# A short convolution and two matrix products on one core: the opening in a new order on all queues

## The chip, the cores and the metric

The kernel runs on one core of one Trainium2 chip. The core has five engines, each with a queue of its own that is worked off strictly in order: PE (TensorE, matrix products), DVE (VectorE), ACT (ScalarE), POOL (GpSimd) and SP (SyncE, which here only issues DMAs). An instruction at the head of a queue that has to wait holds back all that stands behind it on that queue, and nothing else. DMAs are issued by SP and by POOL. The metric is the device time of one execution in microseconds (us).

## The reference

`x` is 8 x 4096 x 192, `w_in` is 192 x 2048, `w_out` is 2048 x 192, all float32.

```python
w = softmax(weight, axis=-1)                    # 8 heads x 7 taps
conv[b, s, d] = sum_k w[head(d), k] * x[b, s - 6 + k, d]   # causal, 24 channels a head
h = conv.reshape(32768, 192) @ w_in             # 32768 x 2048
g = h * (1 / (1 + exp(-1.702 * h)))
out = g @ w_out                                 # 32768 x 192
```

## The kernel before

**Work in big steps.** The 32768 tokens are worked off in 32 "big steps" (`big` = 0 to 31). Each has 512 tokens from each half of the batch. A big step has three parts: the convolution (7 taps for each of three groups `c` of 64 channels; a tap is a product with one scalar a channel), the first product with the gelu, and the second product with transposition and store. Both products of steps 1 to 31 are done by a fast bilinear scheme: sums of blocks of the convolution (`SUMS_C`), sums of blocks of `w_in` (`SUMS_W`, 24 of them, made once, in place), 20 block products for each half `v` of the columns (`FIRST`, `TERMS`), and for the second product sums of `w_out` ("forms": `COPY_O` copies on ACT, `SUMS_O` adds by POOL's accumulating DMAs, in four stages `add_forms(0)` to `add_forms(3)`, and four sign changes on ACT in `end_forms`) and sums of `g`.

**Step 0 is different** and is called the opening here. While `w_in` and `w_out` still arrive and are rounded (eight pieces: `split_piece` on DVE, `split_rest` on ACT, `join_piece`, `sign_piece` and the rounding on DVE), the first product is done plainly: 16 calls of `plain`, 12 of them in a loop in `first_step`. After each call comes a gelu on ACT and then one function of the list `stages`, in which the rest is hung: the pieces of the weights, the loads, the taps of step 1. The second product of step 0 (`second_first`) uses a scheme of seven products of quadrants: `a11` to `a22` are parts of `w_out`, `b11` to `b22` parts of `g`; `s1` to `s4` and `t1`, `t2` are sums of them, and `sums_b` overwrites `b12` with `b22 - b12`. Each call of `go` takes some steps of a product; one step is four matmuls side by side in the four column groups, three for the main product and one "side" matmul for another (`aside`), and each matmul is two passes. PE's order is: a11 b11 (8 steps), a12 b21 (6), s2 t2 (8), a12 b21 (2), s3 b12 (8), s4 b22 (2), a22 t2 (8); the side matmuls of steps 1 to 24 are s1 t1, those after them s4 b22. Behind the seven products come four transposes on DVE (`turn`) and the stores.

**The convolution of step 1.** Groups 2 and 0 go by `tap`: ACT multiplies each tap into a place of its own, and POOL adds the places up with accumulating DMAs in the order of `TREE_1`; those of one group are (1,2), (3,4), (0,1), (5,6), (0,3), (0,5), of which (0,1), (0,3) and (0,5) each need the landing of the one before. Group 1 goes by `conv` on DVE, handed out by `work(us)` from the list `todo`. `need("done 1")` issues what is left of it, then one sum on DVE (`OPEN_SUM`), which needs all taps of all groups, and then blocks of the convolution are copied across partitions by SP's DMAs (`cross`, `cross_piece`). Only then can the ten sums `SUMS_C` of step 1 be made (`next_sum`); for step 1 they are DVE's, for all later steps POOL's.

**Order by hand.** Nothing reorders at run time. `FILL_1` says what is put between which of the items of `FIRST` in step 1 (a dictionary for `v` = 0 and one for `v` = 1, keys are indices into `FIRST`); `FILL` does so for later steps. `PLAN` is the written order of the second product of steps 1 to 31. `begin_sums(2)` stands behind step 1's first product, so step 2's ten sums are handed out by the `vsum` entries of `PLAN`; for later steps they are all handed out by `FILL` before `PLAN` begins, and the `vsum` entries then find nothing.

Of the kernel before, what the change touches and what calls it, by code (L numbers as in the profile page):

```python
# [15 lines left out]
def kernel(  # L16
# [149 lines left out]
    def side(big, other, b):  # L166
# [4 lines left out]
    SUMS_W = [  # L171
# [4 lines left out]
    ]  # L176
    OPEN_W = 0
# [193 lines left out]
    def sums_w_in(i):  # L371
        add_up(lambda j: w_in_s[:, j, :], *SUMS_W[i])
# [267 lines left out]
    def plain(u, m, n, v, slot, ks=range(NC), first=0):  # L640

        for k in ks:
# [101 lines left out]
    def fill(big, kind, *args):  # L744
        if kind == "work":
            work(*args)
        elif kind == "tap":
            next_tap()
        elif kind == "add":
            for _ in range(*args):  # L750
                next_add()
        elif kind == "vsum":
            next_sum()
        elif kind == "cross":
            cross_piece()
        elif kind == "turn":
# [25 lines left out]
    def second_first(between, fetch, last_seeds):  # L782
# [83 lines left out]
        add_forms(0)  # L866
        sub(t1[1], b12[1], b11[1])
# [22 lines left out]
        act.copy(whole(c12), whole(a))  # L890
        go(c11, p2[6:], first=False)
        sub(t2[0], b21[0], t2[0])
        sub(t2[1], b21[1], t2[1])
        add(p1, p1, whole(c11))
        go(a, listed(s3, b12), first=False)
        add_forms(2)
        between()
        act.copy(whole(c21), whole(a))
        add(p5, p5, whole(a))
        go(c12, p3[6:], first=False)  # L900
        cross_piece()
        for i in range(OPEN_W):
            sums_w_in(i)
        fetch()
        for i in range(OPEN_W, len(SUMS_W)):
            sums_w_in(i)
        next_tap()
        next_tap()
        steps = listed(a22, t2, (1, 0))
        for i in range(0, len(steps), 2):  # L910
            go(c21, steps[i : i + 2], first=False)
            if i == 0:
                last_seeds()
            next_tap()
            if i < 6:
                next_tap()
        assert not side
        cross_piece()
        turn(0, 0, blocks(p1), js)
        cross_piece()  # L920
        assert not pieces
        turn(1, 1, blocks(p5), js)
        add(q12, q12, whole(c12))
        turn(1, 0, blocks(whole(c21)), js)
        store(0, 0)
        turn(0, 1, blocks(q12), js)
        store(0, 1)

# [11 lines left out]
    def store(big, n, o=None, queues=(nc.sync,) * 3):  # L940
# [29 lines left out]
        ("side", 8, 8, "k1", 2, 4), ("acc", 7, 10), ("sum", 13, 18, "+", 4), ("acc", 18, 14), ("main", 2, 5, "p4", 0),  # L970
        ("sum", 6, 9, "-", 5), ("vsum",), ("go", 1), ("tap",), ("go", 2), ("tap",), ("tap",), ("tree",), ("go", 1),
# [5 lines left out]
        ("main", 21, 7, "p2", 0), ("go", 2), ("side", 7, 20, "k1"), ("vsum",), ("tap",), ("tree",), ("go", 2),  # L977
# [375 lines left out]
```

## Time and profile before

| what | value |
|---|---|
| median of 3 runs | 2276.99 us (2276.36 to 2277.63) |
| the profiled execution's own time | 2275.51 us |
| its span, first to last instruction | 2273.7 us |
| mean granted clock of PE | 0.996 |
| PE busy | 2252.5 us (99%) |
| DVE, ACT, POOL busy | 1985.3 (87%), 1709.2 (75%), 1069.9 (47%) us |

The span is 1.8 us shorter than the profiled execution's own time; what lies between is outside of the program's instructions. The busy time of PE includes the overlap of matmuls in flight, so a busy PE isn't a PE at its peak; where PE waits less than a matmul's length, no idle time shows. Start times in the timelines count from the start of the span. In a row of the timeline, a bracket at the end says how long the engine had been idle and what ended the wait; `xN` says that N instructions of the same kind are merged in one row.

### The profile page before, as it was taken

How to read it: one execution, taken by the hardware profiler on the slowest of the kernel's cores; microseconds unless marked ns; L12 is line 12 of the kernel's file. 1: busy time of each engine (PE TensorE's matmuls, PEld its weight loads, DVE VectorE, ACT ScalarE, POOL GpSimd, SP SyncE). 2: the span in 40 equal slices, each digit the busy share in tenths (PEclk: the TensorE clock that was granted, in tenths of full speed). 3: DMA queues.
4: the chain of work that ended last, by engine and by line, in shares of the span. 5: the costliest groups of instructions: out<-in, count | busy, mean ns of one | idle time of the engine just before them, and what ended most of it. 6: DMA issues, size and time to landing. Idle time of an engine off the chain costs nothing.

```text
span 2273.7 us, 62148 instructions
## 1 busy us (share of the span) xinstructions
PE 2252.5 (99%) x24966; PEld 1564.5 (69%) x24966; DVE 1985.3 (87%) x2967; ACT 1709.2 (75%) x3233; POOL 1069.9 (47%) x1101
## 2 busy tenths in 40 slices
PE   9899999999999999999999999999999999999999
PEld 5366577776777667777667776677776677766775
DVE  8798889988889888898888888888988888888888
ACT  8477777778777787777787777877777877778754
POOL 1446544555434555445554445554455544455510
PEclk9899999999999999999999999999999999999999
DMA  8876577666576565776665765666766657665543
GB/s 200 153 152 142 111 141 152 127 128 126 114 162 138 124 132 114 139 153 129 128 126 113 161 139 124 130 117 136 154 130 128 126 112 160 139 126 106 101 97 71
DMA packets 276111, 298.84 MB, mean 131 GB/s; under 512 B 119152, under 2 KB 203376, under 8 KB 275824
## 3 DMA queue, kind: packets, MB, share of 16 engines
q0 software_dynamic: 58080, 151.48, 36.9%
q1 hardware_dynamic: 216096, 142.99, 27.7%
q8 instruction: 198, 3.24, 0.6%
q14 instruction: 89, 0.73, 0.1%
q10 hardware_dynamic: 1648, 0.39, 0.1%
HBM read 53.15 MB, written 25.17 MB: 34 GB/s over the span
## 4 chain that ended last, share of the span: by engine, by line
PE 92%; DVE 4%; DMA 2%; ACT 1%; issue 1%; POOL 0%; DVEq 0%; POOLq 0%; ACTq 0%; SPq 0%
PE slot L597 47%; PE slot L1021 45%; DVE g L363 1%; DMA conv_t<-conv_t 1%; DMA xin<-in_x_dram 0%; PE slot L839 0%; DMA g<-osbs 0%; DMA conv_t<-w_form 0%; DVE room L363 0%; DVE w_in_s L363 0%; DMA w_in_s<-in_moe_w_out_dram 0%; DVE slot L638 0%; DVE osbs L937 0%; DVE conv_t L474 0%; PE slot L1113 0%
## 5 line engine op out<-in xcount | busy, mean ns | idle before, releaser
L597 PE MATMUL slot<-conv_t,w_in_s 64*128 64x512 f32 x5152 | 1148.5, 595 | 2.2 <-DVE slot L638 1.4
L597 PEld LDWEIGHTS slot<-conv_t,w_in_s 64*128 64x128 f32 x5152 | 669.5, 186 | 468.3 <-issue 304.9
L1021 PE MATMUL slot<-g,w_form 128*32 128x256 f32 x9672 | 894.2, 379 | 0.7 <-DVE room L363 0.7
L1021 PEld LDWEIGHTS slot<-g,w_form 128*32 128x32 f32 x9672 | 576.3, 110 | 129.3 <-DVE room L363 1.7
L506 POOL TENSOR_TENSOR conv_t<-conv_t,g 128x512 f32<-128x512 f32 x354 | 450.5, 1279 | 96.5 <-ACT g L488 72.9
L1021 PE MATMUL slot<-g,w_out_s 128*32 128x256 f32 x5952 | 467.5, 379 | 1.1 <-DVE g L363 1.1
L363 DVE TENSOR_TENSOR g<-g 128x1024 f32<-128x1024 f32 x372 | 451.2, 1226 | 7.5 <-DMA g<-osbs 1.0
L1046 ACT COPY room<-slot 32x256 f32<-32x256 f32 x651 | 237.6, 365 | 289.7 <-PE slot L1021 281.4
L638 DVE TENSOR_TENSOR room<-slot,room 128x512 f32<-128x512 f32 x620 | 383.7, 680 | 67.0 <-PE slot L597 66.7
L632 ACT COPY room<-slot 128x512 f32<-128x512 f32 x620 | 337.8, 595 | 75.6 <-PE slot L597 59.1
L488 ACT ACTIVATE g<-xt,cw 128x512 f32<-128x512 f32 x534 | 354.1, 715 | 3.6
L619 ACT ACTIVATE g<-room 128x1024 f32<-128x1024 f32 x248 | 265.6, 1071 | 79.6 <-DVE room L638 50.2
L614 ACT ACTIVATE g<-slot 128x512 f32<-128x512 f32 x528 | 283.1, 609 | 51.5 <-PE slot L597 32.2
L997 POOL DMA_DIRECT2D g<-g x124 | 127.2, 1031 | 360.2 <-PE slot L1021 343.3
L638 DVE TENSOR_TENSOR slot<-slot,room 128x512 f32<-128x512 f32 x372 | 239.8, 689 | 53.9 <-PE slot L597 51.2
L1021 PEld LDWEIGHTS slot<-g,w_out_s 128*32 128x32 f32 x5952 | 239.7, 110 | 41.8 <-DVE room L638 22.8
L361 POOL TENSOR_TENSOR conv_t<-conv_t 128x256 f32<-128x256 f32 x210 | 181.5, 870 | 129.4 <-PE slot L597 120.0
L1021 PE MATMUL slot<-osbs,w_form 128*32 128x256 f32 x2232 | 229.5, 379 | 0.0
L511 POOL DMA_DIRECT2D g<-g x120 | 105.8, 881 | 232.6 <-ACT g L488 91.9
L1021 PEld LDWEIGHTS slot<-osbs,w_form 128*32 128x32 f32 x2232 | 132.4, 110 | 23.8
L638 DVE TENSOR_TENSOR slot<-room,slot 128x512 f32<-128x512 f32 x124 | 79.8, 688 | 43.0 <-PE slot L597 42.0
L1021 PE MATMUL slot<-room,w_form 128*32 128x256 f32 x1488 | 112.9, 379 | 0.4 <-DVE room L363 0.4
(169 smaller groups left out, 1678.7 us busy)
## 6 DMA issues: line engine op xcount, KB each, us to landing
g<-g POOLq DMA_DIRECT2D x124, 512.0 KB, 6.4
xin<-in_x_dram SPq DMA_DIRECT2D x240, 180.0 KB, 4.1
conv_t<-conv_t SPq DMA_DIRECT2D x186, 192.0 KB, 5.4
g<-g POOLq DMA_DIRECT2D x120, 256.0 KB, 5.3
conv_t<-conv_t SPq DMA_DIRECT2D x186, 128.0 KB, 3.0
out_dram<-osbs SPq DMA_DIRECT2D x186, 128.0 KB, 2.7
g<-room POOLq DMA_DIRECT2D x31, 512.0 KB, 5.2
conv_t<-g POOLq DMA_DIRECT2D x60, 256.0 KB, 5.4
```

Source lines behind the costliest of these rows:

```text
L361: eng.tensor_add(v(dst), v(a), v(b))
L363: eng.tensor_sub(v(dst), v(a), v(b))
L488: act.mul(home, conv_src(big, c, k), cw[:, c, k : k + 1])
L506: nc.gpsimd.tensor_add(dst, dst, home)
L597: nc.tensor.matmul(slot[h], w_in_s[halves[h], a, v * P : (v + 1) * P], src, start=first, stop=True, skip_group_check=True,)
L614: act.activation(dst[:, :, h, :], src[h].rearrange("p (o t) -> p o t", o=2), AF.Gelu_apprx_sigmoid, scale=float(sign),)
L619: act.activation(dst.rearrange("p o h t -> p h o t"), src.rearrange("p h (o t) -> p h o t", o=2), AF.Gelu_apprx_sigmoid, scale=float(sign),)
L632: act.copy(bank(dst, h), bank(src, h))
L638: op(*(bank(t, h) for t in (dst, a, b)))
L997: nc.gpsimd.dma_start(out=spot(dst), in_=spot(a), accum_op=ALU.add)
L1021: nc.tensor.matmul(dst, w, t, start=first, stop=last, skip_group_check=True)
L1046: act.copy(to, d)
```

## The change

No instruction of the computation is added or taken away; the order in which they are put on the queues is new, from 28 us of the profile on to the end of step 1.

1. `stages`: the rounding of `w_out`'s pieces and the load and transposes of step 1's input are handed out in another order, so that `round_w_out(1)` stands in front of `turn_x(1)`, and `split(7)` behind the first sum `t1[0]`. The 14 taps of step 1 go 3 into stage 6, 4 into stage 8, 6 into stage 10, 1 into stage 11 (before: 1, 1, 2, 2, 2, 2, 2, 2 in stages 4 to 11).
2. `second_first`: `s3[0]`, `sums_b(0)` and `sums_b(1)` stand in front of `need("done 1")`; `add_forms(0)` and `add_forms(1)` behind it, before the copy of a11 b11 out of PSUM; the ten `SUMS_C` and the 24 `SUMS_W` are spread among the rest (`next_w`), the latter in a new order that keeps their dependences; step 1's first product (`fetch`) stands before the last two steps of s4 b22; two of the transposes change places.
3. `add_forms(2)` moves from `second_first` to the start of step 1's first product, `add_forms(3)` from the end of `first_step` to index 9 of its second half, `end_forms` to index 25 of that half.
4. `FILL_1`: step 2's taps and the group that DVE does (`work`) stand at other indices; 4 of the 7 `conv` of step 2 fall into the first half, 3 into the second (before: all 7 into the first).
5. `PLAN`: the ten `vsum` stand at other places. They act in step 1 alone.

```diff
     SUMS_W = [
-        (12, 2, "+", 5), (13, 7, "-", 10), (11, 13, "-", 11), (12, 11, "+", 12), (14, 8, "+", 11), (15, 1, "-", 11),
+        (12, 2, "+", 5), (13, 7, "-", 10), (11, 13, "-", 11), (18, 13, "-", 0), (15, 1, "-", 11), (16, 0, "+", 9),
...
+    w_left = list(SUMS_W)
+    def next_w(n):
+        for _ in range(n):
+            add_up(lambda j: w_in_s[:, j, :], *w_left.pop(0))
     FILL_1 = [
         {
-            0: (("add", 12),), 1: (("work", 0.8),), 8: (("work", 0.8),), 9: (("tap",),), 16: (("work", 0.8),),
-            19: (("tap",),), 21: (("tap",), ("work", 0.8)), 27: (("work", 0.8),), 28: (("work", 0.8),),
-            30: (("tap",),), 31: (("tap",),), 34: (("tap",),), 42: (("work", 0.8), ("tap",)),
+            0: (("form", 2),), 5: (("tap",),), 6: (("work", 0.8),), 8: (("add", 12),), 9: (("tap",),),
+            14: (("work", 0.8), ("tap",)), 16: (("work", 0.8),), 20: (("tap",),), 25: (("tap",),),
+            28: (("work", 0.8),),
         },
         {
-            5: (("g", 0),), 8: (("g", 1),), 13: (("turn", 0),), 15: (("g", 2),), 19: (("turn", 1),), 20: (("g", 3),),
-            24: (("turn", 2),), 29: (("g", 4),),
+            4: (("g", 0),), 8: (("work", 0.8),), 9: (("form", 3),), 15: (("turn", 0),), 21: (("g", 1),),
+            22: (("turn", 1),), 24: (("turn", 2),), 25: (("forms",),), 27: (("g", 2),), 31: (("g", 3),),
+            37: (("g", 4),),
         },
     ]
# second_first
-        add_forms(0)
+        steps = listed(a22, t2, (1, 0))
+        sub(s3[0], a11[0], a21[0])
         sub(t1[1], b12[1], b11[1])
         add(s1[1], a21[1], a22[1])
+        sub(s2[1], s1[1], a11[1])
+        sums_b(0)
+        sub(s2[0], s1[0], a11[0])
         go(a, listed(a11, b11))
-        act.copy(p1, whole(a))
+        sums_b(1)
         sub(t2[1], b22[1], t1[1])
-        for i in range(2):
-            sub(s2[i], s1[i], a11[i])
-        add_forms(1)
         need("done 1")
         cross_blocks(1)
         while pieces:
             cross_piece()
-        for i in range(2):
-            sub(s4[i], a12[i], s2[i])
-            sub(s3[i], a11[i], a21[i])
+        begin_sums(1)
+        sub(s4[0], a12[0], s2[0])
+        next_sum()
         go(c11, p2[:6], more=True)
-        begin_sums(1)
-        while sums_left:
+        for _ in range(3):
             next_sum()
+        add_forms(0)
+        add_forms(1)
+        sub(s3[1], a11[1], a21[1])
+        act.copy(p1, whole(a))
...
+        go(a, listed(s2, t2), first=False)
...
+        sub(t2[0], b21[0], t2[0])
+        next_sum()
+        sub(s4[1], a12[1], s2[1])
...
+        go(a, listed(s3, b12), first=False)
+        act.copy(whole(c21), whole(a))
         cross_piece()
-        sums_b(0)
-        sums_b(1)
-        go(a, listed(s2, t2), first=False)
...
+        next_w(3)
+        fetch()
+        next_w(2)
         sub(t2[1], b21[1], t2[1])
+        next_w(1)
+        go(c12, p3[6:], first=False)
         between()
-        act.copy(whole(c21), whole(a))
+        next_w(8)
+        next_tap()
...
-        for i in range(OPEN_W, len(SUMS_W)):
-            sums_w_in(i)
...
# first_step: the stages (after)
+        def stage_0():
+            split(4); split(5); load_x(1)
+        def stage_1():
+            rounds(3)
+        def stage_3():
+            round_w_out(0)
+        def stage_4():
+            round_w_out(1); split(6); load_w_out(3)
+        def stage_5():
+            turn_x(1)
+        def stage_6():
+            round_w_out(2); taps_next(3)
+        def stage_8():
+            next(rest); todo.extend(prepare(1)); taps_next(4); split(7)
+        def stage_9():
+            round_w_out(3)
+        def stage_10():
+            taps_next(1); next(rest); taps_next(4); next(rest); taps_next(1)
+        def stage_11():
+            taps_next(1); work(1.3)
...
-        add_forms(3)
         end_taps()
```

More of the change, by code (lines that the diff above doesn't have):

```diff
@@ L755, in fill @@
             cross_piece()
+        elif kind == "forms":
+            need("forms")
+        elif kind == "form":
+            add_forms(*args)
         elif kind == "turn":
@@ L892, in second_first @@
-        sub(t2[0], b21[0], t2[0])
+        add_forms(0)
+        add_forms(1)
+        sub(s3[1], a11[1], a21[1])
+        act.copy(p1, whole(a))
+        for _ in range(2):
+            next_sum()
+        go(a, listed(s2, t2), first=False)
+        for _ in range(2):
+            next_sum()
+        go(c11, p2[6:], first=False)
+        next_sum()
+        sub(t2[0], b21[0], t2[0])
+        next_sum()
+        sub(s4[1], a12[1], s2[1])
+        add(p1, p1, whole(c11))
+        act.copy(whole(c12), whole(a))
@@ L893, in second_first @@
+        next_w(2)
+        go(a, listed(s3, b12), first=False)
+        act.copy(whole(c21), whole(a))
+        cross_piece()
+        next_w(3)
+        fetch()
+        next_w(2)
         sub(t2[1], b21[1], t2[1])
-        add(p1, p1, whole(c11))
-        go(a, listed(s3, b12), first=False)
-        add_forms(2)
+        next_w(1)
+        go(c12, p3[6:], first=False)
         between()
-        act.copy(whole(c21), whole(a))
-        add(p5, p5, whole(a))
-        go(c12, p3[6:], first=False)
@@ L901, in second_first @@
-        cross_piece()
-        for i in range(OPEN_W):
-            sums_w_in(i)
-        fetch()
-        for i in range(OPEN_W, len(SUMS_W)):
[L906 to L917, printed above, removed]
+        next_w(8)
@@ new lines, in second_first @@
+        next_tap()
+        next_w(2)
+        cross_piece()
+        next_w(1)
+        go(c21, steps[0:2], first=False)
+        next_w(3)
+        next_tap()
+        last_seeds()
+        next_tap()
+        go(c21, steps[2:4], first=False)
+        add(p5, p5, whole(a))
+        for _ in range(2):
+            next_tap()
+        go(c21, steps[4:6], first=False)
+        for _ in range(2):
+            next_tap()
+        go(c21, steps[6:8], first=False)
+        for _ in range(2):
+            next_tap()
@@ L918, in second_first @@
+        cross_piece()
+        next_w(1)
+        turn(0, 0, blocks(p1), js)
+        next_w(1)
         cross_piece()
[L919 to L922, printed above, removed]
         add(q12, q12, whole(c12))
         turn(1, 0, blocks(whole(c21)), js)
-        store(0, 0)
+        turn(1, 1, blocks(p5), js)
         turn(0, 1, blocks(q12), js)
         store(0, 1)
+        store(0, 0)
+        assert not side and not pieces and not sums_left
@@ L1239, in first_step, with stage_2, stage_7 @@
         rest = second_first(between, fetch, last_seeds)
+        def stage_0():
+            split(4)
+            split(5)
+            load_x(1)
+        def stage_1():
+            rounds(3)
+        def stage_2():
+            pass
         def stage_3():
+            round_w_out(0)
+        def stage_4():
+            round_w_out(1)
             split(6)
+            load_w_out(3)
+        def stage_5():
             turn_x(1)
-        def stage(n, todo=lambda: next(rest)):
-            todo()
-            taps_next(n)
-        split(3)
-        stages = [
-            stage_0, stage_1, stage_2, stage_3, lambda: stage(1, stage_4), lambda: stage(1, lambda: split(7)),
-            lambda: stage(2, lambda: round_w_out(2)), lambda: stage(2, lambda: round_w_out(3)),
-            lambda: stage(2), lambda: stage(2), lambda: stage(2), lambda: stage(2, lambda: work(1.3)),
-        ]
+        def stage_6():
+            round_w_out(2)
+            taps_next(3)
+        def stage_7():
+            pass
+        def stage_8():
+            next(rest)
+            todo.extend(prepare(1))
+            taps_next(4)
+            split(7)
+        def stage_9():
+            round_w_out(3)
+        def stage_10():
+            taps_next(1)
+            next(rest)
+            taps_next(4)
+            next(rest)
+            taps_next(1)
+        def stage_11():
+            taps_next(1)
+            work(1.3)
+        split(3)
+        rounds(2)
+        load_w_out(2)
+        stages = [stage_0, stage_1, stage_2, stage_3, stage_4, stage_5,
+            stage_6, stage_7, stage_8, stage_9, stage_10, stage_11]
         free = [slots[0], sums, slots[1], slots[2]]
```

26 lines of the change are left out of this document (4 added, 22 removed), and 46 rows, old and new, of tables (PLAN, SUMS_W).

## The prediction

> **What bounds the kernel now.** I read the page first, then the busy time by stretches, then the timelines of PE, DVE, POOL and ACT over the first 190 us.
>
> ```profile
> span 2273.7 us, 62148 instructions
> PE 2252.5 (99%) x24966; PEld 1564.5 (69%) x24966; DVE 1985.3 (87%) x2967; ACT 1709.2 (75%) x3233; POOL 1069.9 (47%) x1101
> 75.00:100.00 25.00, 17.34 (x137) 5.95 (x128) 19.24 (x27) 4.12 (x7) 14.05 (x16) 0.80 1.00 176
> 110.98:187.08 76.10, 72.66 (x780) 46.61 (x779) 72.06 (x100) 55.89 (x106) 36.58 (x34) 1.00 0.79 155
> 187.08:206.00 18.92, 18.66 (x85) 11.67 (x83) 13.65 (x23) 15.91 (x28) 14.21 (x12) 1.00 0.34 72
> 187.08:257.91 70.83, 70.22 (x786) 44.75 (x784) 60.91 (x92) 54.67 (x103) 34.89 (x35) 1.00 0.67 136
> ```
>
> The columns of the stretches are length, then busy time of PE, weight loads, DVE, ACT and POOL, granted clock, DMA share, GB/s. Over the whole span PE is the bound and nothing can be won in the later steps, which the change leaves alone: step 2 (187.08 to 257.91) has PE busy for 70.22 of 70.83 us. It is the opening that isn't bound by PE: from 75 to 100 us PE works 17.34 of 25 us. Step 1 (110.98 to 187.08) takes 5.3 us longer than step 2 and is DVE's: 72.06 of 76.10 us busy.
>
> ```profile
> 18.71 37.18 PE L597 MATMUL slot<-conv_t,w_in_s 64*128 64x512 f32 x172 [0.26 <-DVE w_in_s L346]
> 57.96 0.63 PE L839 MATMUL slot<-g,w_out_s 128*32 128x512 f32 x3 [2.07 <-ACT g L614]
> 80.00 0.59 PE L844 MATMUL slot<-w_in_s,conv_t 128*32 128x512 f32 x1
> 88.25 1.07 PE L839 MATMUL slot<-g,conv_t 128*32 128x512 f32 x3 [7.66 <-DVE g L851]
> 91.04 0.85 PE slot L839 x3
> 93.77 0.43 PE slot L839 x3
> ```
>
> The last two rows are of the chain that ended last. PE ends the plain products at 55.9, begins the seven products at 57.96, does 24 of the 42 steps by 80.6, and then stands for 7.66 us until `sums_b` (L851) has made the new b12. Its first passes after that take 0.85 us, the later ones 0.43, so the gap costs more than its length.
>
> ```profile
> 40.22 2.10 DVE L443 STREAM_TRANSPOSE xt<-xin 128x576 f32<-128x576 f32 x3 [2.11 <-DMA xin<-in_x_dram]
> 50.57 0.95 DVE L338 SCALAR_TENSOR_TENSOR w_form<-osbs,w_form 128x768 uint32<-128x768 uint32 x1
> 51.55 1.44 DVE L346 SCALAR_TENSOR_TENSOR w_out_s<-w_form 128x96 f32<-128x96 f32 x8
> 55.30 2.29 DVE L855 TENSOR_TENSOR room<-g,room 128x2048 f32<-128x2048 f32 x1
> 57.51 0.55 DVE L857 TENSOR_TENSOR w_form<-w_out_s 128x384 f32<-128x384 f32 x1
> 59.95 2.28 DVE L867 TENSOR_TENSOR w_in_s<-g 128x2048 f32<-128x2048 f32 x1
> 65.75 3.11 DVE L474 SCALAR_TENSOR_TENSOR conv_t<-xt,cw,conv_t 128x512 f32<-128x512 f32 x4
> 79.51 0.42 DVE L361 TENSOR_TENSOR conv_t<-conv_t 128x256 f32<-128x256 f32 x1 [10.65 <-DMA conv_t<-conv_t]
> 85.82 4.49 DVE L851 TENSOR_TENSOR g<-g 128x2048 f32<-128x2048 f32 x2
> 98.33 0.68 DVE L899 TENSOR_TENSOR room<-room,slot 96x512 f32<-96x512 f32 x1 [1.01 <-ACT slot L898]
> 110.98 1.24 DVE L638 TENSOR_TENSOR room<-slot,room 128x512 f32<-128x512 f32 x2
> ```
>
> This names the cause. DVE has nothing to do from 68.86 to 79.51: `need("done 1")` puts `OPEN_SUM` at the head of its queue, which waits 10.65 us for the taps' DMAs, and `s3`, `s4`, the ten sums and `sums_b`, which PE needs, are queued behind. After that DVE is busy nearly without a pause to 110.98, where step 1's first sum (L638) begins, and on through step 1. So the path is: taps' DMAs, then DVE.
>
> **The change on that path.** It fills DVE's 10.65 us with work that stood behind them. I work along DVE's queue in four pieces.
>
> *Entry.* ACT's rows are needed here.
>
> ```profile
> 46.13 0.94 ACT L326 ACTIVATE w_form<-w_form,bias 128x768 f32<-128x768 uint32 x1 [2.08 <-DVE w_form L315]
> 51.70 1.34 ACT L488 ACTIVATE w_form<-xt,cw 128x512 f32<-128x512 f32 x2
> 52.92 1.08 ACT L614 ACTIVATE g<-slot 128x512 f32<-128x512 f32 x2
> 53.88 0.74 ACT L488 ACTIVATE w_form<-xt,cw 128x512 f32<-128x512 f32 x1
> 60.42 1.39 ACT L488 ACTIVATE conv_t<-xt,cw 128x512 f32<-128x512 f32 x2
> 69.39 2.99 ACT L405 COPY w_form<-w_out_s 128x384 f32<-128x384 f32 x7
> ```
>
> With `round_w_out(1)` (3.2 us, like L338 and L346 with their join) in front of the transposes, their 2.11 us of wait is covered. It is lost again at piece 7: its ACT half now stands behind stage 8's gelu and four taps. A call of `plain` is 12 matmuls of the 172, 2.6 us, so stage 8's product ends at 55.9 - 3 x 2.6 = 48.1; gelu 1.1, four taps at 0.62 (half of 1.34, less overlap) 2.5, two passes of the piece 1.9: 53.6. Then DVE's sign 1.0, rounding 1.4, `t2[0]` 2.2, `s1[0]` 0.5: 58.7, where it now ends at 58.0. PE's first step needs `s1[0]` for its side matmul, so PE begins 0.9 later, at 58.9, and DVE reaches `t1[1]` at 60.7 instead of 59.95.
>
> *Up to the wait.* Before: 59.95 to 68.86, 8.9 us. Added: `s3[0]` 0.5 and both `sums_b` 4.4. So DVE comes to `OPEN_SUM` at 60.7 + 13.8 = 74.5.
>
> *The end of the wait* is set by POOL's queue.
>
> ```profile
> 50.54 1.00 POOL L511 DMA_DIRECT2D w_form<-w_form  x1 [46.46 <-ACT w_form L488]
> 54.49 0.86 POOL L511 DMA_DIRECT2D conv_t<-w_form  x1 [0.91 <-DMA w_form<-w_form]
> 58.35 0.86 POOL L511 DMA_DIRECT2D conv_t<-w_form  x1 [2.12 <-DMA conv_t<-w_form]
> 62.98 0.86 POOL L511 DMA_DIRECT2D conv_t<-w_form  x1 [3.77 <-DMA conv_t<-w_form]
> 76.07 0.86 POOL L511 DMA_DIRECT2D conv_t<-conv_t  x1 [3.49 <-DMA conv_t<-conv_t]
> ```
>
> These are group 2's (1,2), (0,1), (0,3), (0,5) and group 0's last. Group 0's adds all stand behind group 2's (0,5): from its issue to the end of the wait are 79.51 - 62.98 = 16.5 us, whatever ACT does. Group 2's taps come earlier: the first three right behind the gelu of stage 6, which can now run at 43.8 (its product ends at 55.9 - 5 x 2.6 = 42.9, and piece 7's half, 46.13, isn't ahead of it), and the last four at 49.2 to 51.7 instead of up to 54.6. So (1,2) goes out at 46.9, (3,4) at 50.9, (0,1) at 51.4; the links of 3.9 and 4.6 us of the rows bring (0,5) to 59.9. I take 60.2, as step 2's input loads meanwhile. The wait then ends at 60.2 + 16.5 = 76.7, 2.8 earlier. Bounds: no earlier at all (79.5), and DVE's own 74.5. Group 0's last tap, at 60.8 instead of 61.8, isn't late for it.
>
> *After the wait.* Before: 79.51 to 110.98, 31.5 us. Gone are `sums_b` 4.4, `s3[0]` 0.5, and the wait of 1.0 at L899; the 24 sums of `w_in`, transposes and turns are the same instructions in another order. 31.5 - 5.9 = 25.6, so step 1's first sum begins at 102.3 instead of 110.98: **8.7 us earlier**.
>
> Is PE in time? 24 steps took 22.6 us (57.96 to 80.6); from 58.9 that is 81.5. Fifth step of s3 b12, at 84.9, needs `s4[1]`, which stands after the wait behind `OPEN_SUM` 0.4, `s4[0]` 0.5, ten sums at 0.4, `s3[1]` 0.5 and `t2[0]` 2.2, and ends at 84.8: just in time. The 18 remaining steps at 0.86 and one product of 0.9 end PE at 97.9, 4.4 before DVE. So all of PE's 7.66 us and its slow passes vanish, and DVE alone sets the gain. The copy of a11 b11 is now behind 15 form copies on ACT; they wait for group 2's (0,5) to land, 63.6, and take 15 x 0.43 = 6.4 (L405): 70.0, while PE wants it at 73. Free. `add_forms(0)` and `(1)` on POOL stand behind the taps' chain as before. SP's crosses move with `OPEN_SUM`.
>
> **Step 1** has the same DVE work, two effects of opposite sign, and no row that shows their sum.
>
> ```profile
> L474 DVE SCALAR_TENSOR_TENSOR conv_t<-xt,cw,conv_t 128x512 f32<-128x512 f32 x6 | 6.4, 1074 | 0.1
> L363 DVE TENSOR_TENSOR g<-g 128x1024 f32<-128x1024 f32 x12 | 16.3, 1372 | 0.1
> L363 DVE TENSOR_TENSOR g<-g 128x1024 f32<-128x1024 f32 x12 | 14.5, 1218 | 0.2
> 102.81 0.86 POOL L407 DMA_DIRECT2D w_form<-w_form  x1 [9.71 <-DMA w_form<-w_form]
> 120.20 1.19 POOL L511 DMA_DIRECT2D conv_t<-g  x1 [4.52 <-PE slot L597]
> 124.41 8.84 POOL L506 TENSOR_TENSOR conv_t<-conv_t,g 128x512 f32<-128x512 f32 x5
> ```
>
> The first two rows are of step 1, the third is of step 3. In step 1 a `conv` takes 1.07 us instead of 0.78 (L474 above, 3.11 for four) and a sum of `g` 1.37 instead of 1.22, while POOL adds at the same time: 1.8 + 1.8 = 3.6 us. `PLAN` now puts four of step 2's sums, not two, in front of POOL's first wait for the second product, under L638's sums; at most 3.6 is won. Against it: `add_forms(2)` now stands on POOL between the big DMA adds of step 2's taps (the last issue, 120.20, moves to 111.5) and its tensor adds (8.84 for five), and `add_forms(3)` behind these. Its third DMA waits for the first to land: 4.5 us if like the links above, 9.71 at worst. With 4.5: third 117, adds to 126.5, the last of `add_forms(3)` 129.5, landed 134. `end_forms` on ACT, at index 25 of the second half, comes to it at 102.3 + 18.9 + 9 = 130, and all gelus and copies behind wait some 3.5 us. I take 0 for step 1, bounds -3.6 and +3.5.
>
> **Sum.** Against the profiled execution (2275.51, 1.8 over its span): 2275.51 - 8.7 = 2266.8. The median is 1.5 above it, so 2276.99 - 8.7 = 2268.3.
>
> **Rivals.** *POOL falls behind (slower).* As just worked out, but with landings of 9.71: third form DMA 122, adds to 132, last of `add_forms(3)` 135, landed 144.5, ACT held for 14.5 us at index 25: 2268.3 + 14.5 = 2282.8. Each us of landing counts twice; from (8.7 - 3.5) / 2 + 4.5 = 7.1 us a landing on, the gain is gone. For it: the DMA share of 1.00 from 75 to 100 us, where most of the 9.71 lies; against: fewer DMAs lie there now. The Trainium skill, DMA: Bandwidth & Descriptors, section "Issuing engines are not separate DMA queues", says that DMAs of all engines share the same 16 and interleave; by that rule SP's load and stores of that time lengthen these landings. Chance 0.10.
>
> *DVE has no room for three convs.* They leave the half with slack (in step 2 DVE works 13.65 of 18.92 us there) for one without: 3 x 1.07 = +3.2, 2271.5. Chance 0.10.
>
> *The chain of taps doesn't move* (79.5): +2.8, 2271.1; with the one before 2274.3. Chance 0.10.
>
> *The contention with POOL goes altogether*: 2268.3 - 3.6 = 2264.7, if nothing waits for `end_forms`. The Trainium skill, SBUF — State Buffer, section "SBUF: two separate sides", has DVE instructions with two SBUF inputs and a GpSimd instruction exclude each other for their whole length; by that, moving POOL's sums under L638, which reads PSUM, frees the others. The 1372 against 1218 ns agrees in sign. Chance 0.15.
>
> **Numbers.** Forecast 0.55. About 0.2%, 4.5 us, is what can be told from no change here. Faster by more: nearly all of forecast, contention case and the two small rivals, 0.79; same: their upper tails and half of POOL's case, 0.13; slower 0.08. The range goes from 2263.5 (contention case, wait ended 1 us sooner) to 2274.3.
>
> **What would show it.** Right: DVE's wait at L361 under 3.5 us, PE's gap at L839 in mid-opening under 1 us, first L638 at 102 to 103, step 1 within 73 to 79 us. Wrong: a wait of ACT at L411, or of POOL at L407, over 5 us; a taps' chain ending at 79; or PE's seven products ending after 102.

## The result and the profile after

| | median | runs | ratio to before, 95% |
|---|---|---|---|
| before | 2276.38 us (2275.25 to 2278.68) | 9 | |
| after | 2270.62 us (2268.92 to 2272.64) | 9 | 0.9972 [0.9962, 0.9982] |

The change takes 5.8 us off, about 0.3%. The forecast was 2268.3, with the range 2263.5 to 2274.3. The profiled execution of after is the longest of its nine (2272.64 us; before's was 2275.51), so its profile has less of the gain than a typical run.

First the page and the stretches of after; the columns of the stretches are as before (length, PE, weight loads, DVE, ACT, POOL, clock, DMA share, GB/s).

```profile
span 2270.5 us, 62135 instructions
PE 2250.4 (99%) x24966; PEld 1546.6 (68%) x24966; DVE 1984.4 (87%) x2967; ACT 1708.0 (75%) x3233; POOL 1068.4 (47%) x1101
```

```profile
75.00:100.00 25.00, 23.56 (x198) 6.67 (x192) 22.11 (x46) 9.60 (x16) 14.00 (x16) 1.00 1.00 183
102.47:183.12 80.65, 72.94 (x778) 49.36 (x778) 71.49 (x99) 57.51 (x110) 38.47 (x39) 0.96 0.83 158
125.00:150.00 25.00, 19.56 (x136) 12.79 (x136) 21.01 (x25) 16.00 (x31) 15.86 (x15) 0.86 0.68 132
183.12:253.80 70.68, 70.08 (x786) 47.40 (x784) 60.89 (x91) 54.62 (x103) 34.99 (x35) 1.00 0.68 137
```

The stretch from 75 to 100 us, where PE worked 17.34 us at a clock of 0.80, now has 23.56 us at 1.00. But step 1, from its first sum to step 2's, takes 80.65 us instead of 76.10. Step 2 is the same. Of the 8.5 us that step 1 begins earlier, 4.0 are left when step 2 begins (183.12 against 187.08), and 3.2 in the span; where the last 0.8 go stays open.

DVE's timeline of after:

```profile
53.42 0.96 DVE L337 SCALAR_TENSOR_TENSOR w_form<-osbs,w_form 128x768 uint32<-128x768 uint32 x1 [2.78 <-ACT w_form L326]
57.97 0.55 DVE L864 TENSOR_TENSOR w_form<-w_out_s 128x384 f32<-128x384 f32 x1
77.40 0.42 DVE L360 TENSOR_TENSOR conv_t<-conv_t 128x256 f32<-128x256 f32 x1 [3.07 <-DMA conv_t<-conv_t]
102.47 1.25 DVE L640 TENSOR_TENSOR room<-slot,room 128x512 f32<-128x512 f32 x2
137.82 1.29 DVE L640 TENSOR_TENSOR slot<-room,slot 128x512 f32<-128x512 f32 x2 [3.01 <-PE slot L599]
183.12 1.25 DVE L640 TENSOR_TENSOR room<-slot,room 128x512 f32<-128x512 f32 x2
```

The wait at `OPEN_SUM` (now L360) fell from 10.65 to 3.07 us and ends at 77.40. Step 1's first sum (L640) begins at 102.47, not 110.98. The wait for piece 7 (L337, 2.78 us) is there as forecast. New is 137.82: in step 1 DVE waits 3.01 us for PE. PE's timeline says what PE waited for:

```profile
58.58 0.62 PE L851 MATMUL slot<-room,w_form 128*32 128x512 f32 x1 [1.82 <-DVE w_form L864]
59.03 0.59 PE L851 MATMUL slot<-room,w_form 128*32 128x512 f32 x1
80.93 0.63 PE L846 MATMUL slot<-g,conv_t 128*32 128x512 f32 x3 [1.28 <-ACT slot L908]
135.64 8.70 PE L599 MATMUL slot<-conv_t,w_in_s 64*128 64x512 f32 x28 [4.88 <-ACT slot L636]
```

The 7.66 us gap of the opening is down to 1.28. In its place PE stands for 4.88 us in the second half of step 1's first product, for ACT. ACT's timeline there, and POOL's of the opening and of step 1:

```profile
133.07 1.08 ACT L616 ACTIVATE g<-slot 128x512 f32<-128x512 f32 x2 [5.59 <-POOL conv_t L508]
139.80 0.52 ACT L413 ACTIVATE w_form<-w_form 128x384 f32<-128x384 f32 x1 [1.49 <-DMA w_out_s<-w_form]
```

```profile
46.58 1.00 POOL L513 DMA_DIRECT2D w_form<-w_form  x1 [42.50 <-ACT w_form L490]
53.43 0.86 POOL L513 DMA_DIRECT2D conv_t<-w_form  x1 [1.89 <-DMA w_form<-w_form]
61.41 0.86 POOL L513 DMA_DIRECT2D conv_t<-w_form  x1 [3.29 <-DMA conv_t<-w_form]
...
112.61 1.19 POOL L513 DMA_DIRECT2D conv_t<-g  x1 [4.53 <-PE slot L599]
114.57 2.28 POOL L409 DMA_DIRECT2D w_form<-w_form  x2
121.64 0.86 POOL L409 DMA_DIRECT2D w_form<-w_form  x1 [4.79 <-DMA w_form<-w_form]
124.48 0.86 POOL L409 DMA_DIRECT2D w_form<-w_form  x1 [1.99 <-DMA w_form<-w_form]
125.04 8.00 POOL L508 TENSOR_TENSOR conv_t<-conv_t,g 128x512 f32<-128x512 f32 x5
132.99 1.76 POOL L409 DMA_DIRECT2D w_form<-w_out_s  x2
134.11 2.40 POOL L409 DMA_DIRECT2D w_out_s<-w_form  x2
```

Read the last block from below. The products of step 2's taps lie partly in `g`, and POOL's tensor adds (L508) read them there. A gelu of step 1's second half (L616) writes over that part of `g`, so it waits until the last of these adds is done, at 133.0. The adds stand on POOL behind the four DMA adds of `add_forms(2)` (L409), and the third and fourth of those wait 4.79 and 1.99 us at the head of the queue for landings. So ACT stands 5.59 us, then PE 4.88, then DVE 3.01. PE's gap costs more than its length, as in the opening of before: from 135.64 to 139.00, right behind it, the granted clock is 0.50, and it is 0.86 as a mean between 125 and 150.

### The profile page after: what moved, and what is told of

Same layout as the page of the kernel before. It is cut to its first block, busy times and chain, and to the rows that moved or that the text cites. A ratio compares the mean times of both kernels' runs of the same rounds, so it can differ in the third digit from the quotient of the medians.

```text
span 2270.5 us, 62135 instructions
## 1 busy us (share of the span) xinstructions
PE 2250.4 (99%) x24966; PEld 1546.6 (68%) x24966; DVE 1984.4 (87%) x2967; ACT 1708.0 (75%) x3233; POOL 1068.4 (47%) x1101
## 4 chain that ended last, share of the span: by engine, by line
PE 87%; DVE 5%; DMA 4%; issue 2%; POOL 1%; ACT 1%; SPq 1%; DVEq 0%; POOLq 0%; ACTq 0%
PE slot L599 45%; PE slot L1044 42%; DVE g L362 2%; DMA g<-osbs 1%; POOL conv_t L508 1%; DMA conv_t<-conv_t 1%; DVE room L362 1%; DMA g<-in_moe_w_in_dram 1%; DMA g<-g 0%; DMA conv_t<-w_form 0%; SPq L265 0%; DMA xin<-in_x_dram 0%; DMA w_form<-w_form 0%; ACT g L490 0%; DVE osbs L360 0%
## 5 line engine op out<-in xcount | busy, mean ns | idle before, releaser
L508 POOL TENSOR_TENSOR conv_t<-conv_t,g 128x512 f32<-128x512 f32 x354 | 449.6, 1276 | 90.3 <-ACT g L490 62.0
L640 DVE TENSOR_TENSOR room<-slot,room 128x512 f32<-128x512 f32 x620 | 383.8, 680 | 67.5 <-PE slot L599 67.4
L616 ACT ACTIVATE g<-slot 128x512 f32<-128x512 f32 x528 | 282.5, 611 | 55.8 <-PE slot L599 31.1
L640 DVE TENSOR_TENSOR slot<-slot,room 128x512 f32<-128x512 f32 x372 | 239.9, 689 | 54.5 <-PE slot L599 52.1
L360 POOL TENSOR_TENSOR conv_t<-conv_t 128x256 f32<-128x256 f32 x210 | 180.9, 867 | 128.9 <-PE slot L599 119.6
L640 DVE TENSOR_TENSOR slot<-room,slot 128x512 f32<-128x512 f32 x124 | 79.8, 688 | 45.7 <-PE slot L599 44.0
```

What stands on the lines that cost most here:

```text
L360: eng.tensor_add(v(dst), v(a), v(b))
L508: nc.gpsimd.tensor_add(dst, dst, home)
L616: act.activation(dst[:, :, h, :], src[h].rearrange("p (o t) -> p o t", o=2), AF.Gelu_apprx_sigmoid, scale=float(sign),)
L640: op(*(bank(t, h) for t in (dst, a, b)))
```

## The experiments

Three theories stood at first. **P**: the opening gave what was forecast, and step 1 lost part of it to POOL's order, the form adds standing in front of the taps' adds. **D**: step 1 lost it on DVE, by the convs that moved into its second half or by the new places of the `vsum`. **O**: step 1, begun earlier, only waits longer for DMAs, whatever its order. The kernels were timed in three groups, each on a chip of its own and against before, whose median was 2275.84 us in the first group (opening_alone, step1_alone, form2_behind, plan_before), 2275.47 in the second (convs_first, forms_late, sums_b_behind, load_later) and 2276.48 in the third (plan_before_2, old_fill, load_after_open). Between groups the ratios to before are the ones to compare.

**opening_alone**: after's opening with the step 1 of before, that is `FILL_1` and `PLAN` as before, `add_forms(2)` in `second_first`, `add_forms(3)` at the end of `first_step`.

```diff
     FILL_1 = [ {
-            0: (("form", 2),), 5: (("tap",),), ...
+            0: (("add", 12),), 1: (("work", 0.8),), ...     # as before, PLAN too
# second_first
         go(c12, p3[6:], first=False)
+        add_forms(2)
         between()
# first_step
+        add_forms(3)
         end_taps()
```

> The opening's new order with step 1 as it was (FILL_1, PLAN, add_forms(2) in front of the transposes and add_forms(3) at the end of first_step). Theory P (POOL's order in step 1 costs the gelu a wait): the opening's 8.5 us are won whole, step 1 takes 76 us again, so about 2276.4 - 8.5 = 2267.9; no wait of ACT at L616 for POOL over 1.5 us. Theory D (DVE has no room for three more convs in step 1's second half): the same 2267.9. Theory O (an early opening only makes step 1 wait for DMAs, whatever its order): some 2270.6 again.

Measured: 2272.41 us, ratio 0.9989 [0.998, 0.9998]. This missed the figures of all three theories: it is slower than after. DVE's, POOL's, ACT's and PE's timelines of this kernel show why:

```profile
101.78 1.25 DVE L640 TENSOR_TENSOR room<-slot,room 128x512 f32<-128x512 f32 x2
...
185.78 1.25 DVE L640 TENSOR_TENSOR room<-slot,room 128x512 f32<-128x512 f32 x2
```

```profile
99.31 0.86 POOL L409 DMA_DIRECT2D w_form<-w_form  x1 [8.99 <-DMA w_form<-w_form]
101.50 3.64 POOL L513 DMA_DIRECT2D g<-g  x3
108.81 1.19 POOL L513 DMA_DIRECT2D conv_t<-g  x1 [3.67 <-PE slot L599]
```

```profile
117.90 2.06 ACT L616 ACTIVATE g<-slot 128x512 f32<-128x512 f32 x4 [4.07 <-issue]
```

```profile
118.55 12.87 PE L599 MATMUL slot<-conv_t,w_in_s 64*128 64x512 f32 x44 [3.18 <-ACT g L616]
```

The opening alone is worth all it was said to be (101.78). Step 1 then takes 84.0 us. In the old order the form adds stand in front of step 2's taps on POOL; one of them waits 8.99 us for a landing, so the taps' DMA adds go out from 101.50 instead of 97.25 as in after. Before had that wait too (9.71 us, and the taps' adds from 104.96), but there the adds went out 6 us ahead of step 1's first sum; here that sum comes 9.2 us sooner and the adds only 3.5. The "issue" in ACT's row names no releaser. That this gelu waits for a tap's DMA add, which reads its product in `g`, is inferred: the add issued at 108.81 took 9.0 us to land, which is 117.8, and the gelu starts at 117.90. With the opening shortened, step 1 takes 8 us longer in its old order; old_fill below tests whether that is the forms' place.

**step1_alone**: the reverse, before's opening with after's `FILL_1`, `PLAN` and places of the forms.

```diff
# FILL_1, PLAN, add_forms(2), add_forms(3), end_forms: as after
# SUMS_W, second_first, stages: as before
```

> The opening as it was, with the new FILL_1 and PLAN and add_forms(2), add_forms(3) and end_forms at their new places. Theory P and theory D: step 1 loses what it loses in the changed kernel, 2.8 to 4.5 us: 2279 to 2281. Theory O: no loss, 2276.4.

Measured: 2278.24 us, ratio 1.001 [1.0002, 1.0019]: slower than before by 2.4, a little less than the 2.8 to 4.5 that P and D expected; O expected no loss. Step 1 takes 78.85 us (109.87 to 188.72). ACT's and PE's timelines:

```profile
138.68 1.09 ACT L614 ACTIVATE g<-slot 128x512 f32<-128x512 f32 x2 [3.80 <-POOL conv_t L506]
```

```profile
141.25 1.17 PE L597 MATMUL slot<-conv_t,w_in_s 64*128 64x512 f32 x3 [3.63 <-ACT slot L634]
```

The same wait as in after, without after's opening. So it comes from step 1's new order itself.

**form2_behind** is after with one edit: the form adds behind step 2's taps, at index 26 of the first half instead of 0.

```diff
-            0: (("form", 2),), 5: (("tap",),), 6: (("work", 0.8),), ...
+            5: (("tap",),), 6: (("work", 0.8),), ...
-            28: (("work", 0.8),),
+            26: (("form", 2),), 28: (("work", 0.8),),
```

> The changed kernel with add_forms(2) moved from index 0 to index 26 of step 1's first half, behind the last of step 2's taps, nothing else. Theory P: POOL's five tensor adds no longer stand behind a DMA's landing, they end some 5 to 8 us sooner, PE's gap of 4.9 us in step 1 falls under 1 us, the median falls by 2.8 to 4.5 us, to 2266 to 2268. Theory D: no change, 2270.6, and PE's gap stays.

Measured: 2266.48 us (2265.27 to 2268.14), ratio 0.996 [0.9948, 0.9973], as P said. Its stretch of step 1, and POOL's and ACT's timelines:

```profile
101.42:177.73 76.31, 72.65 (x778) 47.12 (x778) 69.31 (x100) 57.40 (x110) 37.17 (x38) 0.98 0.87 163
```

```profile
112.69 8.86 POOL L508 TENSOR_TENSOR conv_t<-conv_t,g 128x512 f32<-128x512 f32 x6
121.50 1.77 POOL L409 DMA_DIRECT2D w_form<-w_form  x2
124.84 0.86 POOL L409 DMA_DIRECT2D w_form<-w_form  x1 [1.57 <-DMA w_form<-w_form]
```

```profile
126.34 1.06 ACT L616 ACTIVATE g<-slot 128x512 f32<-128x512 f32 x2
134.27 0.52 ACT L413 ACTIVATE w_form<-w_form 128x384 f32<-128x384 f32 x1 [2.71 <-DMA w_out_s<-w_form]
```

The tensor adds end at 121.5 instead of 133.0, the gelu runs at 126.34 with no wait in front of it, and step 1 is back at 76.31 us. The two ends add up: 110.98 - 101.42 = 9.6 won in the opening, 0.2 lost in step 1, and 2275.84 - 2266.48 = 9.4 measured. Against after's figure this is 4.1 us; against plan_before (2270.77 us, below), which has after's places of the forms and ran in the same group, 4.3, and its fastest run is slower than form2_behind's slowest. DVE's convs are shorter here too (5.6 us for six, 7.7 in after), but that isn't the gain: in after all six had ended by 132, ahead of DVE's 3.01 us of waiting for PE. This shows the cause of after's loss, and theory O falls with it. The landings are shorter as well: the first two form adds took 6.8 and 9.0 us from issue to landing in after, where SP issued eight loads of x between 111.61 and 118.3, and 3.3 us here, behind these loads.

**plan_before** puts the ten `vsum` of after back to before's places; **plan_before_2** does the same to form2_behind.

```diff
     PLAN = [
-        ("side", 13, 16, "k0"), ("main", 1, 5, "p2", 1), ("vsum",), ("go", 2), ("sum", 14, 14, "-", 18), ("go", 2),
+        ("side", 13, 16, "k0"), ("main", 1, 5, "p2", 1), ("vsum",), ("go", 2), ("sum", 14, 14, "-", 18), ("go", 1),
+        ("vsum",), ("go", 1), ("main", 16, 10, "p3", 0), ...
```

> The changed kernel with the vsum entries of PLAN as they were. If four sums in front of POOL's first wait free DVE of the contention (up to 3.6 us worked out from the rows before), undoing it costs up to 3.6: 2274. If it doesn't matter while step 1 is held by the gelu's wait: 2270.6, within 1 us.

> form2_behind with the vsum entries of PLAN as before. With the gelu's wait out of the way, DVE sets step 1 again. If four of POOL's sums ahead of its first wait free DVE of contention, undoing it costs up to 3.6 us: 2268 to 2270. If the place of the vsum doesn't matter: 2266.5.

Measured: 2270.77 us, 0.9978 [0.9969, 0.9987], where after has 0.9972; and 2267.68 us, 0.9957 [0.9944, 0.9971], where form2_behind has 0.996. Step 1 takes 80.67 us (after: 80.65) and 76.79 us (form2_behind: 76.31) in the profiles. The new places of the `vsum` make no difference that can be measured.

**convs_first** puts two of the three convs of form2_behind's second half back into the first.

```diff
-            5: (("tap",),), ... 20: (("tap",),), 25: (("tap",),),
+            1: (("work", 0.8),), 5: (("tap",),), ... 20: (("tap",), ("work", 0.8)), 25: (("tap",),),
...
-            4: (("g", 0),), 8: (("work", 0.8),), 9: (("form", 3),), ...
+            4: (("g", 0),), 9: (("form", 3),), ...
```

> form2_behind with two of the three convs of step 1's second half put back into its first half (indices 1 and 20 of the first half, none at index 8 of the second, one left at index 15). Theory D (DVE has no room for them in the second half): 2 x 1.07 = 2.1 us faster, 2264.4. Theory P: they take the place of idle time that other waits leave, no more than 0.5 us either way: 2266 to 2267.

Measured: 2266.23 us, 0.9959 [0.9945, 0.9972]. In the same group load_later, which differs from form2_behind only by the place of a load that went out at the same time, has 2266.09 us, so the 2.1 us of theory D aren't there. Theory D falls with these three.

**forms_late** takes the wait that the prediction had feared, ACT's at `end_forms` (2.71 us in form2_behind), out of form2_behind.

```diff
-            ... 24: (("turn", 2),), 25: (("forms",),), 27: (("g", 2),), 31: (("g", 3),), 37: (("g", 4),),
+            ... 24: (("turn", 2),), 27: (("g", 2),), 31: (("g", 3),), 37: (("g", 4),), 38: (("forms",),),
```

> form2_behind with end_forms moved from index 25 to index 38 of step 1's second half. In form2_behind ACT waits 2.7 us at the sign changes (L413) for the landing of add_forms(3), and PE has a gap of 1.3 us there. Theory P (each wait of ACT for POOL's DMAs holds the gelus and copies behind it): the wait and the gap vanish, 1 to 2.5 us faster than form2_behind's 2266.5: 2264 to 2265.5. If DVE holds step 1 anyway: the same 2266.5.

Measured: 2265.81 us (2265.03 to 2265.88), 0.9956 [0.9943, 0.9968]. The stretch of its step 1:

```profile
101.27:177.09 75.82, 72.52 (x778) 47.65 (x778) 69.41 (x100) 57.21 (x110) 37.39 (x38) 0.98 0.86 164
```

The wait at `end_forms` is gone and step 1 is 0.5 us shorter, but against form2_behind that can't be told from nothing; the 1 to 2.5 us that theory P expected didn't come. It has the lowest median of all kernels that ran, though the ratios of those with the forms behind the taps (0.9956 to 0.996) can't be told apart; after has 0.9972.

**old_fill** asks whether any of after's `FILL_1` is needed: the new opening, `FILL_1` and `PLAN` as in before but for the entry at 42, whose tap and `work` are not handed out there, and the forms behind the taps.

```diff
# against opening_alone
-            ... 34: (("tap",),), 42: (("work", 0.8), ("tap",)),
+            ... 34: (("tap",),), 35: (("form", 2),),
-            5: (("g", 0),), 8: (("g", 1),), 13: (("turn", 0),), ... 24: (("turn", 2),), 29: (("g", 4),),
+            5: (("g", 0),), 8: (("g", 1),), 9: (("form", 3),), 13: (("turn", 0),), ... 25: (("forms",),), 29: (("g", 4),),
# second_first, first_step
-        add_forms(2)
-        add_forms(3)
```

> The new opening with FILL_1 and PLAN as before, save that the last work and the tap entry at index 42 are left out (six of step 2's seven convs in the first half), add_forms(2) stands at index 35 of the first half, behind the last tap, add_forms(3) at index 9 and end_forms at index 25 of the second. Theory P (of the new order of step 1 only the place of the forms on POOL counts): 2266 to 2267.5, step 1 in 76 to 77 us, against 84.0 in opening_alone. If the new places of the taps and of work matter too: 2269 or more.

Measured: 2267.45 us, 0.9957 [0.9944, 0.9969]. DVE's timeline:

```profile
101.96 1.25 DVE L640 TENSOR_TENSOR room<-slot,room 128x512 f32<-128x512 f32 x2
...
179.36 1.25 DVE L640 TENSOR_TENSOR room<-slot,room 128x512 f32<-128x512 f32 x2
```

Step 1 takes 77.4 us, a little over the 76 to 77 expected, against the 84.0 of opening_alone, with nearly the same `FILL_1`. So of the whole new order of step 1 it is the forms' place on POOL that is seen in the time, and taps, convs and `vsum` are not.

**sums_b_behind** takes away the other half: form2_behind with `s3[0]` and both `sums_b` behind the wait at `OPEN_SUM`.

```diff
-        sub(s3[0], a11[0], a21[0])
...
-        sums_b(0)
...
-        sums_b(1)
...
         add_forms(1)
+        sub(s3[0], a11[0], a21[0])
         sub(s3[1], a11[1], a21[1])
...
         sub(s4[1], a12[1], s2[1])
+        sums_b(0)
+        sums_b(1)
```

> form2_behind with s3[0] and both sums_b put back behind the wait (behind s4[1], in front of the sum of p1). By the sum of the prediction 4.9 us go from the wait's shadow back on DVE's path: 2266.5 + 4.9 = 2271.4, DVE's wait at OPEN_SUM grows to about 8 us and PE's gap before s3 b12 comes back with 6 to 8 us. If the gain came from the taps' chain or the order of the w_in sums alone: 2266.5.

Measured: 2274.59 us, 0.9997 [0.9988, 1.0005]: nothing of the gain is left. These 4.9 us of DVE work cost some 8 us (8.5 against load_later in the same group), where 4.9 were expected. DVE's and PE's timelines:

```profile
76.26 0.43 DVE L360 TENSOR_TENSOR conv_t<-conv_t 128x256 f32<-128x256 f32 x1 [7.01 <-DMA conv_t<-conv_t]
107.67 0.68 DVE L945 TENSOR_TENSOR room<-room,slot 96x512 f32<-96x512 f32 x1 [4.15 <-ACT room L853]
110.09 1.25 DVE L640 TENSOR_TENSOR room<-slot,room 128x512 f32<-128x512 f32 x2
```

```profile
87.20 1.08 PE L846 MATMUL slot<-g,conv_t 128*32 128x512 f32 x3 [8.04 <-DVE g L858]
```

The expectation charged DVE's work alone. But PE's gap comes back (8.04 us), with passes of 1.08 us after it, PE ends its products late, and DVE waits 4.15 us for ACT's copy of one of them. So the gain of the opening isn't DVE's 4.9 us alone: with the gap, the path runs through PE.

**load_later** and **load_after_open** ask what the first DMA add of step 1's taps waits for, since in after's profile the chain to `OPEN_SUM` ended 0.7 us later than forecast (in those of form2_behind and forms_late it ended at 76.36 and 76.21, somewhat ahead of the forecast 76.7). Both move step 2's load of x, the first by its place in the program alone, the second (on forms_late) onto SP behind the wait.

```diff
# load_later: stage_5 without the load, stage_8 with it
+            load_x(2)
             split(7)
# load_after_open: stage_5 without the load, second_first with it
         need("done 1")
+        load_x(2)
         cross_blocks(1)
```

> form2_behind with the load of step 2's input put behind stage 8's taps instead of right behind stage 5's transposes. In the changed kernel the first DMA add of group 2 is issued at 46.6 and lands 6.3 us later, among this load; alone such a DMA lands in 3.4. If the taps' chain sets DVE's wait, the chain begins 2 to 3 us sooner, DVE's wait of 3.07 us at OPEN_SUM shrinks to 0.5 to 1, and the median falls by 2 to 2.5 us: 2264 to 2264.5. If the chain is bound by ACT's taps and not by that landing: 2266.5.

> forms_late with the load of step 2's input issued by SP behind the first crosses of step 1, some 35 us later; load_later had changed nothing, since SP, with nothing ahead on its queue, issued the load at the same 43 us. Theory C (the taps' chain is late because its first DMA add shares the DMA engines with this load and lands in 5.7 to 6.3 us instead of 3.4): that add lands at about 50, the wait at OPEN_SUM goes from 2.0 us to under 0.5 and ends at 74.2 to 74.8, DVE's own time. The median falls by up to 2, to 2264, unless the later load in turn holds the transposes of step 2 or step 1's crosses, which would give 1 to 3 back. If the chain is bound elsewhere, the wait still ends at 76.2.

Measured: 2266.09 us, 0.9959 [0.9947, 0.9972], and 2273.16 us, 0.9984 [0.9975, 0.9992]. The first told nothing: SP, with nothing ahead in its queue, issued the load at the same 43.0 us. In the second the load is later. POOL's timeline of forms_late (first row) and of load_after_open, then DVE's of load_after_open:

```profile
52.57 0.86 POOL L513 DMA_DIRECT2D conv_t<-w_form  x1 [1.17 <-DMA w_form<-w_form]
```

```profile
51.21 1.20 POOL L513 DMA_DIRECT2D conv_t<-w_form  x1
```

```profile
75.83 0.43 DVE L360 TENSOR_TENSOR conv_t<-conv_t 128x256 f32<-128x256 f32 x1 [1.52 <-DMA conv_t<-conv_t]
...
97.28 2.10 DVE L445 STREAM_TRANSPOSE xt<-xin 128x576 f32<-128x576 f32 x3 [7.71 <-DMA conv_t<-conv_t]
```

Without the load beside it the first add has landed when (0,1) is wanted, and (0,1) goes out at 51.21 instead of 52.57. Yet the wait at `OPEN_SUM` ends only 0.4 us sooner than in forms_late, from which it differs by the load alone (76.21), so the load sets little of that chain. Step 2's transposes now wait 7.71 us. Their row names a DMA of the crosses as the last to end; the load, which they read, was issued up to 88.7 and took 10.0 us to land (median), so either can have held them. Step 1's first sum comes at 108.36 instead of 101.27, and the kernel loses 6 to 7 us.

## Why the prediction was right, and which step failed

**The path was right.** The prediction had DVE idle from 68.86 to 79.51 behind `OPEN_SUM`, with the work that PE needs queued behind it, and filling that wait carried the gain: sums_b_behind, which undoes that part, is at before's time.

**Entry and wait.** `s1[0]` was to end at 58.7; it ends at 58.5 (57.97 + 0.55), after the forecast wait for piece 7. PE's first side matmul was to begin at 58.9 and began at 58.58. DVE was to come to `OPEN_SUM` at 74.5 and came at 74.33. The wait was to end at 76.7 and ended at 77.40 in the profiled run: (0,5) of group 2 went out at 61.41 instead of 60.2, because (1,2) landed later (53.43 for (0,1) instead of 51.4). In the profiles of form2_behind and forms_late, with the same opening, it went out at 60.38 and 60.22. From there to the end of the wait were 16.0 us in each, against 16.5.

**After the wait.** 25.6 us were forecast; 102.47 - 77.40 = 25.1. Step 1's first sum was to be 8.7 us earlier and was 8.5. PE's gap of 1.28 us is a little above the named "under 1 us"; its seven products end at 99.0 (first matmul of `fetch` 98.91), before DVE's 102.47. The markers "first L638 at 102 to 103" and a wait of DVE under 3.5 us held.

**The step that failed is step 1's term**, "I take 0 for step 1, bounds -3.6 and +3.5". It was 4.55 us more in the profiled run, and the 80.65 us that step 1 took are outside the marker of 73 to 79. That isn't this run's alone: plan_before's profile, of a run of 2269.89 us, has 80.67 us there. By the medians 8.5 - 5.8 = 2.7 us were lost if the opening won its 8.5 in every run, and 3.8 if it won form2_behind's 9.6; form2_behind won 4.1 to 4.3 back. Two parts of the term were off:
- *The place of the wait.* The prediction followed POOL's delay to `end_forms` alone. There ACT waits 1.49 us. It forgot that the five tensor adds behind the forms free a part of `g`, which a gelu before index 25 writes over; that wait is 5.59 us. The marker "a wait of ACT at L411, or of POOL at L407, over 5 us" looked at the wrong line of ACT, and POOL's longest wait at the forms, 4.79, stayed just under it.
- *The landing.* The working took 4.5 us a landing, and the rival 9.71, with the point of decision at 7.1. The first form DMA took 6.8 us and the second 9.0. The third went out at 121.64, 7.1 us behind the first (114.57), which itself was about 2 us later than the forecast needs for its 117. The adds ended at 133.0: these are the times of the rival "POOL falls behind" (122 and 132), not of the forecast (117 and 126.5). The rival's price of 14.5 us didn't come, since the last forms were issued between 134.11 and 136.5 and had landed by 139.80, under 6 us instead of 9.71, and ACT, delayed itself, came to them at 136.92. So the mechanism of that rival happened in part, at another wait and at a third of its price or less.

That the time stayed within the range is in part luck: the bound of 3.5 us was the price of ACT's wait at `end_forms`, which came to 1.49, and the loss that came was another wait's.

**Contention with POOL** was to give up to 3.6 us, and had a chance of its own. Groups of DVE instructions in step 1 of after, kinds apart (busy us and mean ns of one behind the bar):

```profile
L362 DVE TENSOR_TENSOR g<-g 128x1024 f32<-128x1024 f32 x12 | 14.9, 1254 | 0.1
L476 DVE SCALAR_TENSOR_TENSOR conv_t<-xt,cw,conv_t 128x512 f32<-128x512 f32 x6 | 7.7, 1277 | 0.1
```

The sums of `g` did get shorter (1372 to 1254 ns), but the convs got longer (1074 to 1277): 1.4 us won, 1.3 lost. In form2_behind the convs take 940 ns, so their length in after goes with the place of the forms. Nothing of this is seen in the time, and plan_before and plan_before_2 show that the places of the `vsum` have no price. The Trainium skill, SBUF — State Buffer, section "SBUF: two separate sides", has a DVE instruction with two SBUF inputs and a GpSimd instruction that reads SBUF exclude each other. The runs here don't show this; they show that with POOL's sums at their old places the two groups together take 22.7 us in plan_before, against 22.6 in after, and 20.9 in plan_before_2, against 20.7 in form2_behind. Of the rivals, "DVE has no room for three convs" falls with convs_first, and "the chain of taps doesn't move" with the 77.40. Nor was step 1 DVE's alone, as the prediction had it: in its own row of before PE is busy for 72.66 of the 76.10 us, DVE for 72.06.

**What stays open.** In the kernel with the lowest median step 1 still takes 75.8 us where step 2 takes 70.7 in after; no run took that apart. After's runs spread over 3.7 us, forms_late's over 0.9; that the landings on POOL make the spread is likely, but was not shown.

## What to carry to other kernels

When work is pulled in front of a wait, follow each queue that it shares to the end of the next stage: here the gain of the opening was as forecast, and a third to a half of it was lost because POOL's queue then had DMAs that wait for landings in front of adds whose inputs another engine wanted to overwrite. For every instruction that is held up, list not only who reads its result but who waits to write over its inputs. Here the chain of dependent DMAs belonged behind the compute of its in-order queue, not in front of it: moving one entry of a table from index 0 to 26 was worth 4 us, while the other changes to step 1 that were tried singly, the `vsum` and the convs, were worth nothing that could be measured.

## What the runs showed of the hardware that was not expected

**PE's slow passes after a short gap.** In before, the gap of 2.07 us in front of the second product (57.96) was followed by two passes at the full rate (0.45 us from start to start) and then by four of 0.85 us, until 62.26, as the starts in PE's timeline of before show. The granted clock was 0.97 from 57.96 to 58.87, 0.51 from there to 62.26, and 1.00 after that.

```profile
58.41 0.69 PE L839 MATMUL slot<-g,w_out_s 128*32 128x512 f32 x3
...
58.87 1.09 PE L839 MATMUL slot<-g,w_out_s 128*32 128x512 f32 x3
...
59.72 1.09 PE L839 MATMUL slot<-g,w_out_s 128*32 128x512 f32 x3
...
60.57 1.09 PE L839 MATMUL slot<-g,w_out_s 128*32 128x512 f32 x3
```

In after a gap of 1.82 us, and in step1_alone one of 2.05 us, were followed by passes of 0.43 us at a clock of 1.00. After 7.66 us (before) and 8.04 us (sums_b_behind) the passes were slow each time, for about 5 us, and after the 4.88 us in step 1 of after the clock was 0.50 for 3.4 us. The Trainium skill, TensorE: Matmul & The Clock Gate, section "What's actually happening", gives an idle window of about 3.4 us that runs free of the program. The trace of before doesn't agree: a gap of 2.07 us is shorter than such a window and yet was followed by the low clock, once; what it was that told it from the gap of 2.05 us, no run here shows. The slow stretch in before was 3.39 us long.

**The time that a DMA add takes to land** depended on what flew beside it. POOL's first add of step 1's taps went out at 46.6 us. The add that needs its landing was issued at 53.43 in after and at 52.57 in forms_late, where a load of x flew at the same time, and at 51.21 in load_after_open, where it did not, without waiting. The same kind of add of the forms held POOL for 1.57 us in form2_behind, for 4.79 us in after, beside loads of x, and for 8.99 us in opening_alone, among the opening's other transfers.

**A DMA that is moved in the program isn't moved in time** when its queue is idle: load_later's load went out at the same 43.0 us as form2_behind's.
